# Products of ones through the first search of a transnormer-attention and balanced-MoE kernel

## The chip, the cores and the metric

The kernel runs on one core of one Trainium2 chip. The metric is the device time of one execution in microseconds (us). TensorE (PE in the profile) multiplies, VectorE (DVE) and ScalarE (ACT) work elementwise, GpSimd (POOL) also issues the indirect DMAs, SyncE (SP) issues the other DMAs. "Granted clock" is the share of TensorE's full clock that the profile records as granted.

## The reference

Two blocks follow one another. The first is a linear attention with normalised rows:

```python
kv = np.einsum('bhsd,bhse->bhde', k, v)            # batch 8, heads 8, seq 576, head_dim 64
out = np.einsum('bhsd,bhde->bhse', q, kv)
rms = np.sqrt(np.mean(out * out, axis=-1, keepdims=True) + 1e-06)
x = (out / rms * g_norm)                           # -> 4608 tokens of 512
```

The second gives every token to exactly one of 8 experts, greedily by the largest logit, with room for 576 tokens each:

```python
logits = x @ w_gate                                # [4608, 8]
for idx in np.argsort(-logits.flatten()):
    tok, e = idx // E, idx % E
    if assigned[tok] >= 0 or counts[e] >= cap: continue
    assigned[tok] = e; counts[e] += 1
for e in range(E):
    mask = assigned == e
    out[mask] = np.maximum(x[mask] @ w1[e], 0.0) @ w2[e]
```

## The kernel before, in words

**Attention.** For each of 8 batches `prepare` forms the key-value products (L397) and transposes the queries (L382), and `tiles` makes 4 or 5 tiles of 128 tokens (L481), squares them on ScalarE (L487), copies them out (L488), sums the squares on VectorE (L492), scales (L496 to L500) and reduces the logits (L505, L508). The last tile of the last batch is the end of TensorE's part in this phase. `choice` and `compare_thirds` (L295 to L305, L337) then bring the last quarter of the logits into the form that the search reads.

**PSUM.** The attention's PSUM pool is closed behind this, and a new one is opened for the experts. Its first two tiles are `given_ps` (one bank for all numbers that TensorE gives the search) and `held_ps` (one bank with small tables that VectorE reads). `held_ps` is filled at L598 to L604, which stand outside the hand-written order; VectorE's first instruction there is the copy at L598.

**The first search.** The greedy assignment is done one expert at a time: the largest logit value at which some expert is full is searched, that expert takes its tokens, and so on. The first search cannot lie beside any expert's products, because no expert has tokens yet. `threshold(0, ...)` runs six rounds (`s` from 0 to 5). In a round, TensorE counts for 32 candidate values how many tokens of each expert lie above them: 36 products at L653, one for each block of 128 tokens, with a weight tile of 128 x 32 and a moving tile of 128 x 8. VectorE turns the counts into one number for each candidate (L667, L669), TensorE sums that over the candidates with a matrix of ones and so hands it to all partitions (`kk`, L674), and VectorE works out the next candidates and compares all tokens with them, in three thirds of 12 blocks (L679, L317, L323 in rounds 1 to 3; L696, L337 in rounds 4 and 5), on which the next round's products wait third by third. Beside this, `lowest` has two small pairs of products (L618 behind the number of round 1, L621 behind that of round 2) whose results are needed later. `assign_first` then has two products (L736, L751), and `fetch(0)` makes the list of the first expert's tokens with three products (L919 to L921) and five (L938), from which the indices of the gather come (L950). GpSimd issues the gathers (L959).

**Products of ones.** `ones` (attention) and `warm` (experts) multiply a 128 x 128 tile of ones with a 128 x 512 tile of ones, in bfloat16, into a PSUM bank that nothing reads. Before the change `ones` stands ahead of and within the attention, and `warm(20)` stands behind the five products at L938, `warm(2)` twice behind the first two transposed blocks of tokens.

**Order.** In both blocks `tc.manual_schedule` keeps TensorE, VectorE and ScalarE (in the attention SyncE too) in the order of the program text. All waits between engines are put in by the framework. Each engine works through its own queue in order.

**Behind the search.** The first expert's products (L1149) begin when three gathered blocks of tokens are transposed (L1051) and copied (L1056). From there to the end TensorE works with few gaps, and the later searches lie beside the experts' products.

Of the kernel before, what the change touches and what calls it, by code (L numbers as in the profile page):

```python
# [7 lines left out]
FT = mybir.dt.float32  # L8
# [7 lines left out]
P = 128  # L16
# [10 lines left out]
def kernel(  # L27
# [11 lines left out]
    nc = tc.nc  # L39
# [4 lines left out]
    E, _, F = moe_w1.shape  # L44
# [105 lines left out]
    def small(nm, w=1, dt=FT):  # L150
        return asg.tile([P, w], dt, name=nm, tag="s_" + nm, bufs=2)
# [206 lines left out]
    def ones(times, to=None):  # L358

        if to is None:  # L360
            to = psa.tile([P, 512], FT, name="ones_ps", tag="tr", bufs=2)
        for _ in range(times):
            nc.tensor.matmul(to, lhsT=ones_b, rhs=wide, start=True, stop=True)
# [167 lines left out]
    with tc.manual_schedule(engines={PE, DVE, ACTE, SPE}):  # L531
        ones(18)
        for _ in prepare(0):
            pass
        for b in range(B):
            parts = prepare(b + 1) if b + 1 < B else iter(())
            rows = [((b, j), (b, j + 2)) for j in (0, 1, 4, 5)]
            if b % 2:
                rows.append(((b - 1, R - 1), (b, R - 1)))
            one, scale, logits = tiles(b // 2 * R + b % 2 * (R // 2), rows)  # L540
            copies = []
            if b in choose_at:
                early(*choose_at[b])
            for t in range(len(rows)):
                one(t, copies, {0: 1, 3: 2}.get(t, 0))
                next(parts, None)
                if b < 2 or t == 3 or b == 6 and t == 2:
                    chore()
            for _ in parts:
                pass  # L550
            if b + 1 == B:
                while chores:
                    chore()
            scale()
            logits()
            if b < B - 1:
                chore(2 if b == 6 else 1)

            while len(writes) >= 2 * LAG:
                writes.pop(0)()  # L560
        early(27, GC)
        while chores:
            chore()
        for do in late:
            do()
        while writes:
            writes.pop(0)()
# [35 lines left out]
    for n, x in enumerate((-0.5, 1.0 / QP, 0.0)):  # L603
        nc.vector.memset(one_more[:, n:n + 1], x)  # L604

    deferred = []

    floor = asg.tile([P, 1], FT, name="floor")
# [32 lines left out]
    def threshold(t, over, width, inv, mid):  # L641

        first = t == 0
        exact, ends, cand = first, None, None
        for s in range(NSTEP):
            last = s + 1 == NSTEP
            yield (4.6 if first else 2.8) if s > 0 else 0.4 if first else 2.4

            n_ps = small_ps["n"]
            if first:  # L650

                for c in range(GC):
                    nc.tensor.matmul(n_ps[0:QP, :, 0],  # L653
                                     lhsT=over[c // THIRD][:, c % THIRD],
                                     rhs=best[:, :, c], start=(c == 0), stop=(c == GC - 1))
            else:
                for c in range(0, GC, G):
                    nc.tensor.matmul(n_ps, lhsT=over[:, c:c + G].rearrange("p c n -> p (c n)"), rhs=best[:, :, c:c + G],  # L658
                                     start=(c == 0), stop=(c == GC - G))
            need = goal[0:QP]  # L660
            for g in range(1, 1 if first else G):
                less = small("need", E)[0:QP]
                nc.vector.tensor_tensor(less, need, n_ps[g * QP:(g + 1) * QP, :, g], op=AL.subtract)
                need = less
            full = small("full", E)[0:QP]
            n_full = small("n_full")[0:QP]
            nc.vector.scalar_tensor_tensor(full, in0=n_ps[0:QP, :, 0], scalar=0.0, in1=need, op0=AL.add,  # L667
                                           op1=AL.is_ge, accum_out=n_full)
            nc.vector.scalar_tensor_tensor(some[0:QP], in0=n_full.to_broadcast([QP, 3]), scalar=0.5, in1=one_more,  # L669
                                           op0=AL.is_gt, op1=AL.add)  # L670
            if not first:
                yield 4.0 if t == 1 and s == 0 else 1.7
            kk = small_ps["kk"]
            nc.tensor.matmul(kk, lhsT=ones_b, rhs=some, start=True, stop=True)  # L674
            exact = s + 1 >= DIGITS
            over = None if last else new_over(first)
            if s < DIGITS:
                mid_was, mid = mid, small("mid")
                nc.vector.tensor_scalar(mid, in0=kk[:, 0:1], scalar1=width[:, s:s + 1], scalar2=mid_was, op0=AL.mult, op1=AL.add)  # L679
                if not exact:  # L680
                    d = digits(mid, inv[:, s + 1:s + 2], None if first else small_ps["mx"])
                    if first:
                        for n in range(3):
                            compare_digits(over[n], d, marks, n * THIRD, (n + 1) * THIRD)
                    else:
                        compare_digits(over, d, small_ps["marks"])
                else:
                    lo = small("lo_at")
                    nc.vector.tensor_scalar(lo, in0=mid, scalar1=width[:, NSTEP:NSTEP + 1], scalar2=None, op0=AL.subtract)
            elif not last:  # L690
                ends = small("ends", 2)
                nc.vector.tensor_scalar(ends, in0=kk[:, 1:3], scalar1=width[:, s:s + 1], scalar2=lo, op0=AL.mult, op1=AL.add)
                lo = ends[:, 1:2]
            if exact and not last:
                cand = small("cand", NCAND + 2)
                nc.vector.tensor_scalar(cand[:, 0:NCAND + 1], in0=small_ps["row"], scalar1=width[:, s + 1:s + 2],  # L696
                                        scalar2=lo, op0=AL.mult, op1=AL.add)
                if first:
                    compare_thirds(over, cand)
                else:  # L700
                    compare(over, cand, 0, GC // 2)
                    yield 0.6
                    compare(over, cand, GC // 2, GC)
            if exact and s + 2 == NSTEP:
                nc.vector.tensor_copy(cand[:, NCAND + 1:NCAND + 2], ends[:, 0:1])
            if last:
                got = small("got_ends", 2)
                for n in range(2):
                    at = small("at", NCAND + 1)
                    nc.vector.scalar_tensor_tensor(at, in0=small_ps["row"], scalar=kk[:, 2:3], in1=cand[:, n:NCAND + 1 + n],  # L710
                                                   op0=AL.is_equal, op1=AL.mult, accum_out=got[:, 1 - n:2 - n])
                hi = small("hi")
                nc.vector.tensor_scalar(hi, in0=got[:, 0:1], scalar1=ends[:, 0:1], scalar2=None, op0=AL.min)
            if first:
                next(of_floor, None)
            if deferred:
                deferred.pop(0)()
        tops[t] = hi
        return hi, got[:, 1:2]

    def assign_first(ends):
# [12 lines left out]

        all_ps = small_ps["all"]
        nc.tensor.matmul(all_ps[:, 0:2].rearrange("p t e -> p (t e)"), lhsT=ones_b, rhs=sums, start=True, stop=True)  # L736
        edge = small("edge", GC)
        nc.vector.tensor_tensor(edge, cut[:, 1], cut[:, 0], op=AL.subtract)
        over_room = small_ps["over_room"]
# [9 lines left out]
        index = small("index", dt=I32)  # L749
        nc.vector.tensor_scalar(index, in0=which, scalar1=-1.0, scalar2=float(E), op0=AL.mult, op1=AL.add)  # L750
        nc.tensor.matmul(all_ps[:, 2, 0:1], lhsT=before, rhs=turn_of[:, GC - 1:GC], start=True, stop=True)  # L751
        nc.vector.tensor_tensor(room, room, all_ps[:, 0], op=AL.subtract)
        theirs, left = small("theirs", E), small("left_one")
        nc.vector.scalar_tensor_tensor(theirs, in0=code, scalar=which, in1=room,
# [132 lines left out]
                          mybir.DependencyInfo(mybir.DependencyClass.Sync, mybir.DependencyReason.DATA),  # L887
                          reason="TensorE waits for the tokens")

    def warm(times):  # L890
        w_ps = psm.tile([P, 512], FT, name="warm_ps", tag="y", bufs=2)
        for _ in range(times):
            nc.tensor.matmul(w_ps, lhsT=ones_b, rhs=wide, start=True, stop=True)

    def fetch(t, which, index, later):

        ch = choice() if 0 < t < E - 1 else iter(())
# [21 lines left out]
        nc.tensor.matmul(begin, lhsT=before, rhs=along[:, GC - 1:GC], start=True, stop=True)  # L919
        nc.tensor.matmul(a_ps[:, 1:GC + 1], lhsT=fall, rhs=along, start=True, stop=True)  # L920
        nc.tensor.matmul(a_ps[:, GC + 1:GC + 2], lhsT=prior, rhs=along[:, GC - 1:GC], start=True, stop=True)  # L921
        kn = know[:, t % 2]
        if t == 0:
            nc.scalar.copy(kn[:, 0:GC + 1], a_ps[:, 1:GC + 2])
# [13 lines left out]
            nc.tensor.matmul(s_ps[:, n], lhsT=since[:, n * P:(n + 1) * P], rhs=kn, start=True, stop=True)  # L938
        if t == 0:

            warm(20)
        rel_s = small("rel_s", NB)
        nc.vector.tensor_tensor(rel_s, place_f, s_ps[:, :, GC], op=AL.subtract)
        less = asg.tile([P, NB, GC], FT, name="less", tag="less")
# [388 lines left out]
```

## Time and profile before

| | |
|---|---|
| time, median of 3 runs (lowest, highest) | 655.35 us (655.14, 655.75) |
| the profiled execution: time, span of its instructions | 656.87 us, 655.1 us |
| mean granted clock | 0.964 |
| TensorE busy | 607.8 us (93%) |
| VectorE busy | 385.8 us (59%) |
| ScalarE, GpSimd busy | 195.0 us (30%), 391.1 us (60%) |
| the last products of the attention (L481) | start at 122.51 us |
| the first search, from the first counts to the indices | 125.0 to 154.5 us |
| granted clock 0.50 instead of 1.00 | 37.97 to 44.79 us and 123.30 to 157.43 us |

All times within the profile are counted from the start of the span. A row of the timeline has its start, the length, the engine, the line, the operation, output and inputs, the shapes and the number of instructions that were merged, and in brackets the idle time before it with what ended that. A row of the table of stretches has the stretch, its length, TensorE's busy time (instructions), the granted clock and the DMA engines' load.

### The profile page before, as it was taken

What the parts mean: (1) busy time and instruction counts of PE and PEld (TensorE: products, weight loads), DVE (VectorE), ACT (ScalarE), POOL (GpSimd) and SP (SyncE); (2) the same over time, 40 slices, a digit from 0 to 9 for tenths busy, and PEclk for the clock granted to TensorE, in tenths of its full rate; (3) what the DMA queues carried; (4) which work ended last, traced back from release to release, by engine and by line L of the source; (5) the groups of instructions that cost most, each with busy time, mean ns of one, the idle gap of its engine ahead of it and who ended that gap; (6) DMA issues with size and microseconds to landing.
All of it is one profiled execution on the core that took longest, in us unless ns stands there. A gap on an engine that the chain in (4) does not pass through costs nothing.

```text
span 655.1 us, 12759 instructions
## 1 busy us (share of the span) xinstructions
PE 607.8 (93%) x4922; PEld 467.4 (71%) x4939; DVE 385.8 (59%) x1242; ACT 195.0 (30%) x397; POOL 391.1 (60%) x407
## 2 busy tenths in 40 slices
PE   7889999346999999999999999999999999999994
PEld 4767777343778678867877786778678867877873
DVE  4456767877788678578747955975771153123101
ACT  1545556631331223123212322221223123222310
POOL 1134544204586488659747973887388579848822
PEclk9979999756999999999999999999999999999998
DMA  8998988324506403620631082109104520820001
GB/s 271 315 313 293 309 300 320 126 83 144 185 2 232 137 34 109 220 74 1 213 125 66 2 291 70 42 5 325 41 33 128 203 72 1 292 77 34 0 10 64
DMA packets 49884, 91.02 MB, mean 139 GB/s; under 512 B 3744, under 2 KB 20128, under 8 KB 49824
## 3 DMA queue, kind: packets, MB, share of 16 engines
q1 hardware_dynamic: 43200, 71.31, 31.8%
q0 software_dynamic: 5920, 18.88, 8.4%
q8 instruction: 39, 0.64, 0.4%
q14 instruction: 21, 0.17, 0.1%
q10 hardware_dynamic: 704, 0.02, 0.1%
HBM read 71.32 MB, written 18.87 MB: 138 GB/s over the span
## 4 chain that ended last, share of the span: by engine, by line
PE 77%; DVE 8%; DMA 6%; issue 4%; ACT 2%; POOL 1%; POOLq 0%; SPq 0%; DVEq 0%; ACTq 0%
PE x_ps L1149 13%; PE x_ps L1109 12%; PE z_ps L1149 9%; PE y_ps L1149 9%; PE y_ps L1109 8%; PE z_ps L1109 7%; DMA v_sb<-in_v_dram 4%; PE o_ps L481 4%; PE y_ps L1211 4%; PE t_ps L1051 3%; PE kv_ps L397 3%; PE qt_ps L382 2%; PE given_ps L658 1%; PE given_ps L653 1%; DMA q_sb<-in_q_dram 1%
## 5 line engine op out<-in xcount | busy, mean ns | idle before, releaser
L1154 ACT COPY h<-x_ps 128x288 f32<-128x288 f32 x93 | 37.2, 400 | 166.1 <-PE x_ps L1149 159.7
L1149 PE MATMUL x_ps<-xs,sw 128*128 128x288 f32 x248 | 71.4, 409 | 0.4 <-DVE xs L1064 0.4
L1076 POOL DMA_INDIRECT out_dram<-y_sb,outs x32 | 31.5, 983 | 56.6 <-DVE y_sb L1247 41.1
L1109 PE MATMUL x_ps<-tw,sh 128*128 128x256 f32 x256 | 61.5, 384 | 0.0
L1149 PEld LDWEIGHTS x_ps<-xs,sw 128*128 128x128 f32 x248 | 46.1, 190 | 13.4 <-issue 1.0
L1056 ACT ACTIVATE xt<-t_ps,g_col 128x512 f32<-128x512 f32 (+3 forms) x41 | 25.8, 635 | 91.1 <-PE t_ps L1051 90.9
L1101 POOL TENSOR_TENSOR sh<-hid 128x512 f32<-128x512 f32 x32 | 40.7, 1273 | 19.9 <-ACT hid L1124 19.9
L1109 PEld LDWEIGHTS x_ps<-tw,sh 128*128 128x128 f32 x256 | 47.0, 190 | 7.0 <-issue 0.8
L1037 POOL TENSOR_TENSOR sw<-w_sb 128x256 f32<-128x256 f32 x64 | 46.8, 731 | 7.9 <-PE z_ps L1149 7.5
L513 POOL TENSOR_TENSOR xo<-o_sb,inv 128x512 f32<-128x512 f32 x31 | 32.9, 1091 | 30.7 <-DVE inv L500 17.5
L1124 ACT ACTIVATE hid<-hid 128x576 f32<-128x576 f32 x64 | 43.8, 686 | 22.6 <-DVE hid L1163 12.6
L959 POOL DMA_INDIRECT xg<-x_dram,ids x40 | 37.9, 947 | 15.5 <-issue 9.8
L481 PE MATMUL o_ps<-kvx,qt 64*128 64x72 f32 (+1 forms) x640 | 39.7, 273 | 5.3 <-ACT o_sb L488 3.4
L1187 POOL TENSOR_TENSOR tw<-w_sb 128x512 f32<-128x512 f32 x32 | 40.1, 1277 | 6.5 <-DMA w_sb<-in_moe_w_dram 6.5
L481 PEld LDWEIGHTS o_ps<-kvx,qt 64*128 64x128 f32 (+1 forms) x640 | 34.4, 180 | 12.9 <-issue 8.1
L1149 PE MATMUL z_ps<-xt,sw 128*128 128x288 f32 x128 | 38.0, 414 | 0.0
L1149 PE MATMUL x_ps<-xt,w_sb 128*128 128x288 f32 x124 | 37.3, 415 | 0.5 <-ACT xt L1056 0.5
L1149 PE MATMUL y_ps<-xt,w_sb 128*128 128x288 f32 x128 | 36.8, 408 | 0.0
L1149 PE MATMUL z_ps<-xs,sw 128*128 128x288 f32 x128 | 36.8, 409 | 0.0
L1149 PE MATMUL y_ps<-xs,w_sb 128*128 128x288 f32 x128 | 36.5, 407 | 0.0
L492 DVE TENSOR_REDUCE ms<-sq 128x8 f32<-128x512 f32 x36 | 24.3, 682 | 20.4 <-ACT sq L487 20.1
L425 POOL COPY kvx<-kv 64x512 f32<-64x512 f32 x16 | 9.7, 608 | 44.2 <-DVE kv L419 24.7
(307 smaller groups left out, 1336.1 us busy)
## 6 DMA issues: line engine op xcount, KB each, us to landing
w_sb<-in_moe_w_dram SPq DMA_DIRECT2D x32, 512.0 KB, 5.5
w_sb<-in_moe_w_dram SPq DMA_DIRECT2D x8, 2048.0 KB, 12.6
k_sb<-in_k_dram SPq DMA_DIRECT2D x16, 576.0 KB, 5.5
v_sb<-in_v_dram SPq DMA_DIRECT2D x16, 576.0 KB, 5.9
q_sb<-in_q_dram SPq DMA_DIRECT2D x16, 576.0 KB, 5.6
x_dram<-xo SPq DMA_DIRECT2D x16, 512.0 KB, 4.3
x_dram<-xo SPq DMA_DIRECT2D x4, 256.0 KB, 3.7
xg<-x_dram,ids POOLq DMA_INDIRECT x40, 5.0
```

The lines of the kernel that those rows point to most:

```text
L481: nc.tensor.matmul(o_ps[rows_at, rp, (2 * r2 + l) * W:(2 * r2 + l + 1) * W], lhsT=turned_q[bn][ks, l, block // 2:block // 2 + m].rearrange ...
L513: nc.gpsimd.tensor_tensor(xo[:, t], o_sb[:, t, :, 0:D], inv[:, t * H:(t + 1) * H].rearrange("p (h o) -> p h o", o=1).to_broadcast([P, H, D ...
L959: tokens = nc.gpsimd.indirect_dma_start(out=xg[0:nr], out_offset=None, in_=x_dram, in_offset=bass.IndirectOffsetOnAxis(ap=ids[0:nr, n:n + ...
L1037: in_order(nc.gpsimd.tensor_tensor(o, x, y, op=op))
L1076: put = nc.gpsimd.indirect_dma_start(out=out, out_offset=bass.IndirectOffsetOnAxis(ap=ids_of[t][0:nr, n:n + 1], axis=0), in_=y_sb[0:nr, :] ...
L1101: in_order(nc.gpsimd.tensor_tensor(o[:, ms], x[:, ms], y[:, ms], op=op))
L1109: nc.tensor.matmul(p_ps[:, n], lhsT=left[:, f, n * P:(n + 1) * P], rhs=right[:, f], start=first, stop=(f == FH - 1), skip_group_check=True)
L1124: nc.scalar.activation(both, both, ACT.Relu)
L1149: nc.tensor.matmul(p_ps, lhsT=lhs[:, r], rhs=rhs[:, r], start=(m in (1, 2, 4, 5) and r == 0), stop=(r == 1), skip_group_check=(m in (6, 7, ...
L1154: nc.scalar.copy(u, p_ps)
L1187: in_order(nc.gpsimd.tensor_tensor(o, x, y, op=AL.subtract))
L1211: nc.tensor.matmul(y_ps[l * nr:(l + 1) * nr], lhsT=hid[:, l * FH + f, a:a + nr], rhs=w2[:, l * FH + f, :], start=(f == 0), stop=(f == FH - 1))
```

## The change

`warm` is defined earlier, and both helpers are called at eight places along the first search and its neighbours: seven products behind the last tile of the attention, ten ahead of the last nine counts of round 0, four behind each round's number (nine behind the last), three and five behind the two products of `assign_first`, two behind the three products at L919 to L921, and 24 instead of 20 behind those at L938. Nothing is taken away, and no value that is used changes.

```diff
             if b + 1 == B:
+                ones(7)
                 while chores:
                     chore()
...
+    def warm(times):
+        w_ps = psm.tile([P, 512], FT, name="warm_ps", tag="y", bufs=2)
+        for _ in range(times):
+            nc.tensor.matmul(w_ps, lhsT=ones_b, rhs=wide, start=True, stop=True)
...
                 for c in range(GC):
+                    if s == 0 and c == 27:
+                        warm(10)
                     nc.tensor.matmul(n_ps[0:QP, :, 0],
...
             nc.tensor.matmul(kk, lhsT=ones_b, rhs=some, start=True, stop=True)
+            if first:
+                warm(9 if last else 4)
...
         nc.tensor.matmul(all_ps[:, 0:2].rearrange("p t e -> p (t e)"), lhsT=ones_b, rhs=sums, start=True, stop=True)
+        warm(3)
...
         nc.tensor.matmul(all_ps[:, 2, 0:1], lhsT=before, rhs=turn_of[:, GC - 1:GC], start=True, stop=True)
+        warm(5)
...
         nc.tensor.matmul(a_ps[:, GC + 1:GC + 2], lhsT=prior, rhs=along[:, GC - 1:GC], start=True, stop=True)
+        if t == 0:
+            warm(2)
...
         if t == 0:
-            warm(20)
+            warm(24)
```

More of the change, by code (lines that the diff above doesn't have):

```diff
@@ L888, in behind @@
                           reason="TensorE waits for the tokens")
[L890 to L893, printed above, removed]
     def fetch(t, which, index, later):
```

## The prediction

> **What bounds the kernel now.** I read the page first (slices of the granted clock), then the chain of waits, then the timeline of the search, then a table of stretches. The clock drops only around the first search, and there the chain alternates between engines:
>
> ```profile
> PEclk9979999756999999999999999999999999999998
> ```
>
> ```profile
> 132.03 1.15 PE given_ps L653 x36
> 133.17 0.02 issue
> 133.20 0.17 DVE full L667 x2
> 133.37 0.02 issue
> 133.39 0.16 DVE some L669
> 133.55 0.04 issue
> 133.59 0.18 PE given_ps L674
> ```
>
> Each round is one loop without slack: candidates (L679, L317), first third of comparisons (L323), 36 counts (L653), their sums (L667, L669), the number (L674), candidates again. TensorE's part is 1.15 + 0.18 us of 2.85, all at half clock. What a full clock is worth there is read from the distance between counts, and from the one row of small products that runs at full clock (columns: start, length, engine, line):
>
> ```profile
> 132.03 1.13 PE L653 MATMUL given_ps<-best,over_c 128*32 128x8 bf16 x36 [1.12 <-DVE over_c L323]
> ...
> 164.81 0.38 PE L658 MATMUL given_ps<-best,over 128*128 128x32 bf16 x9
> ```
>
> The flight of one product is 0.175 us in both (175 and 176 ns). So 36 counts at half clock start (1.13 - 0.175) / 35 = 27 ns apart, and nine at full clock (0.38 - 0.176) / 8 = 25 ns apart: almost the same. The number's way is no shorter either: L674 to L679 takes 0.20 us at half clock (130.75 to 130.95) and 0.21 at full (170.11 to 170.32).
>
> When the clock falls and returns is in the table of stretches (start:end, length, TensorE busy, granted clock, DMA share, GB/s). The changes lie on a grid of 3.41 us: 37.97 to 44.79 is two of these, 123.30 to 157.43 ten.
>
> ```profile
> 34.55:37.97 3.42, 2.01 (x46) 1.00 0.92 300
> 37.97:41.38 3.41, 3.41 (x44) 0.50 0.99 324
> 41.38:44.79 3.41, 3.05 (x77) 0.50 1.00 356
> ...
> 116.47:119.89 3.42, 2.55 (x33) 1.00 0.38 145
> 119.89:123.30 3.41, 0.73 (x32) 1.00 0.65 246
> 123.30:126.71 3.41, 0.87 (x27) 0.50 0.02 6
> ...
> 154.02:157.43 3.41, 3.41 (x10) 0.50 0.72 226
> 157.43:160.85 3.42, 3.42 (x21) 1.00 0.64 200
> ```
>
> A stretch busy for 2.01 us lost the clock, one busy for 2.55 us kept it. Busy time counts an eight-column product's whole flight, so I also estimate the time in which columns stream (0.42 ns a bfloat16 column at full clock, twice that in float32, from the 288 columns of L1149 that start 242 ns apart): 0.39 of the stretch that lost it, 0.38 of the one that kept it. Upwards, 1.00 of products of ones brought it back at 157.43, and 0.65 in the first stretch of the kernel (0.42 to 3.83, 2.23 us busy with ones) did not: the ones behind it still start 0.427 apart. A 512-column product of ones takes 0.427 us at half clock (153.509 to 153.936) and 0.216 at full (157.826 to 158.042).
>
> **The change, part by part.** All sums are shifts of the gather's start (155.30). Behind it the chain is a DMA and then TensorE's products, so each us carries to the end.
>
> *Gain of a full clock.* Three rounds of 36 counts fed by L323: 35 x 1.7 ns and 0.02 for the first, 0.08 each. Two rounds fed by L337, whose last third comes late: 0.035 each. The nine counts 0.03, the five at L938 0.04. Sum 0.38 us. Lower bound 0. Upper bound, if 32-column weights went at half of 27 ns: the last third of comparisons then ends last, 0.26 x 3 + 0.16 x 2 + 0.12 + 0.07 = 1.3 us. I take the 25 ns of L658, the only full-clock row of such products.
>
> The Trainium skill, "TensorE: Matmul & The Clock Gate", section "LDWEIGHTS (loading the stationary operand)", estimates a load at its columns / 1.2 ns, with no clock in the formula, so 27 ns for 32 columns; by it this gain is nil.
>
> *Seven behind the last tile.* They start at about 123.1. The stretch that ends at 123.30 is not altered (0.73 us busy), so the clock still falls there: one at 0.216, six at 0.427, the last starts at 125.43 and lands 0.634 later, at 126.07. Who waits for that:
>
> ```profile
> 123.93 0.69 DVE L492 TENSOR_REDUCE ms<-sq 128x8 f32<-128x512 f32 x1 [0.26 <-ACT sq L487]
> 125.01 0.23 DVE L598 COPY held_ps<-rise 128x72 f32<-128x72 f32 x1 [0.39 <-ACT o_sb L488]
> 125.30 0.40 DVE L497 RECIPROCAL inv<-rt 128x40 f32<-128x40 f32 x1
> ```
>
> L598 writes the new pool's second bank, which L488 does not read, yet it waits for the last L488: the whole old pool must be free. The seven use the old pool, so L598 waits for them too, and behind it on VectorE stand L497 to L508, L295 to L305 and L337, the chain up to the nine counts at 129.90. L598 goes at about 126.11 instead of 125.01: 1.10 us. Bounds: 0, if the clock were full (seven end at 124.8, before L488's 124.98) or if the framework puts L598 to L604, which stand outside the manual order, behind L500; 1.10 as the order stands. I take 1.10. The 27 early counts wait as well, 125.03 to 126.2, and have cover.
>
> *Ten ahead of the nine counts.* Ones fill 2.7 us of 123.30 to 126.71, 0.79, between the 0.65 that did not bring the clock back and the 1.00 that did; I take it as back at 126.71. Then the ten end at 129.1, and the nine counts are due at 131.0: nothing. At half clock they would end at 131.2: 0.2.
>
> *Four behind each number.* At full clock 0.86 us, where TensorE waits 1.28 (kk at 133.59 to counts at 134.88): hidden. But does the clock hold? In 130.13 to 133.54 there are four (0.86) and the columns of some 36 counts (0.12): 0.29 of the stretch, below the 0.38 that kept the clock. Busy time, 0.4 + 0.17 + 1.03 + 0.41 with the nine counts at 131.0, is 2.0 us, as much as where it fell. I take it to fall at 133.54, behind the second number.
>
> The Trainium skill, the same page, section "Why this matters for your kernels", says that the clock is lost by idle gaps of over about 3 us. The row differs: 37.97 came after a longest recorded gap of 1.48 us (34.48 to 35.96). By that rule the filled search would stay at full clock, and the sum would be 1.10 - 0.38 = +0.7.
>
> At half clock four take 1.71 us. Behind round 1's number, with L618's two products (2 x 0.22): 2.15 against 1.28, 0.87 late. Round 2, with L621 (0.4): 0.83. Round 3: 1.71 against 1.73, nothing. Round 4: 1.71 against 1.48, but the last third is compared 0.93 after the first, and TensorE catches up: nothing.
>
> *Nine behind the last number.* At full clock 1.94 us against a wait of 2.77 (146.21 to 148.99): hidden. At half 3.84: 1.07 late. The nine are longer than a stretch, so the clock should return within them; between 0 and 1.07 I take 0.70.
>
> *Three, five, two, 24.* L736 to L751 is 1.40 us, L751 to L919 1.74, L921 to L938 0.77. At full clock they take 0.65, 1.08, 0.43: hidden. At half, five cost 0.40 and two 0.1; I take 0. The 24 at full clock end 5.2 us behind L938, the third gathered block came 8.6 behind it (161.55): hidden. Without that cover (half clock) four more cost up to 0.6.
>
> *Sum.* 1.10 + 0.87 + 0.83 + 0.70 = 3.50, less 0.10 of the gain (only a quarter of the search at full clock): +3.4 us. The profiled execution (656.87 us, of which the span is 655.1) would become 660.3. It lies 1.5 us above the median of the runs, 655.35; on that median the sum gives 658.8. Own range of this case: +2.0 (L598 moved behind L500 and part of the nine hidden) to +4.4 (nine in full, five as well), 657.4 to 659.8.
>
> **The rivals.**
>
> *Fill hidden throughout, clock full* (chance 0.16): L598 is placed late or the seven run fast, and a 0.29 share holds the clock. Then -0.38, 655.0; down to 654.0 if counts go at half of 27 ns. This decides from the point at which 130.13 to 133.54 ends at 1.00. For it: at 0.216 each, every run of ones fits into the wait it stands in. Against it: 123.30 falls whatever follows.
>
> *The clock holds, but L598 is late* (0.18): 1.10 - 0.38 = +0.7, 656.1. For it: the flights of counts may count as activity. Against it: the 2.01 us row.
>
> *The clock hardly returns* (0.08): ten cost 0.2, round 0's four 0.43, rounds 1 and 2 as above, nine in full, five 0.40, 24 some 0.5: 1.10 + 0.2 + 0.43 + 0.87 + 0.83 + 1.07 + 0.40 + 0.5 = +5.4, 660.8.
>
> **How the numbers follow.** Likeliest case 0.58: 658.8. 0.2% is 1.3 us, about what a measurement of this kernel can tell from no change. Faster by more needs the first rival and counts at half of 27 ns: 0.07. Within it lie the rest of that rival and the second: 0.27. Slower: 0.58 + 0.08 = 0.66. The range goes from 655.0, the first rival's middle, to 660.0, above the likeliest case's end; outside lie half of the first rival and the third, 0.16.
>
> **What would show it.** Right: L598 starting near 126.1 with TensorE's ones as what ended its wait; a clock of 0.50 in a stretch between 133 and 150; counts of rounds 2 and 3 that start some 2.1 us behind their number, with no wait for VectorE; L736 released by TensorE's queue, not by VectorE. Wrong: L598 at 125.0 or behind L500; 1.00 from 127 on, with counts 13 ns apart; the gather starting before 155.3.

## The result, and the profile after

Over 22 runs of each, the kernel after takes 660.26 us (median; 657.33 to 669.57) and the kernel before 656.30 us (653.52 to 668.98). The ratio is 1.0059, 95% interval 1.0040 to 1.0077: slower by 0.6%, about 3.9 us. The profiled execution of after takes 663.41 us, with a span of 661.5 us.

All of it that belongs to the change lies between the last tile of the attention (L481) and the list's products (L938 before, L947 after; the lines behind L549 have moved): 30.44 us before, 34.56 us after, +4.12 us. From there to the first expert's products it is 9.83 and 9.92 us. From those to the end it is 492.3 us before and 494.7 in this execution of after, but 492.2 to 492.4 us in the profiles of the first five experiments, two of which have exactly after's products behind the list; the 2.4 us are this execution's own.

The page's 40 slices of the granted clock show the same three low slices around the search, with 8, 5 and 8 tenths instead of 7, 5 and 6:

```profile
PEclk9979999858999999999999999999999999999998
```

VectorE's timeline of after, at the point where the attention's PSUM pool is closed:

```profile
123.81 0.69 DVE L492 TENSOR_REDUCE ms<-sq 128x8 f32<-128x512 f32 x1 [0.26 <-ACT sq L487]
125.98 0.24 DVE L599 COPY held_ps<-rise 128x72 f32<-128x72 f32 x1 [1.49 <-PE ones_ps L363]
126.13 0.39 DVE L497 RECIPROCAL inv<-rt 128x40 f32<-128x40 f32 x1
```

The copy now waits for products of ones, and starts 3.60 us behind L481 instead of 2.50. Some 0.14 us of the 1.10 come back just behind it (L497 starts 0.15 us behind the copy, before the change 0.29), so the nine counts are 0.96 late.

TensorE's timeline of after, rounds 0 to 2 and the end of the search:

```profile
123.04 2.83 PE L363 MATMUL ones_ps<-wide,ones_b 128*128 128x512 bf16 x6
...
126.76 2.35 PE L610 MATMUL warm_ps<-wide,ones_b 128*128 128x512 bf16 x10
130.73 0.40 PE L661 MATMUL given_ps<-best,over_c 128*32 128x8 bf16 x9 [1.62 <-DVE over_c L337]
131.57 0.16 PE L682 MATMUL given_ps<-some,ones_b 128*128 128x3 bf16 x1 [0.44 <-DVE some L677]
131.81 0.81 PE L610 MATMUL warm_ps<-wide,ones_b 128*128 128x512 bf16 x3
132.85 1.12 PE L661 MATMUL given_ps<-best,over_c 128*32 128x8 bf16 x36 [0.23 <-DVE over_c L323]
134.41 0.16 PE L682 MATMUL given_ps<-some,ones_b 128*128 128x3 bf16 x1 [0.43 <-DVE some L677]
134.43 1.87 PE L610 MATMUL warm_ps<-wide,ones_b 128*128 128x512 bf16 x4
136.23 0.58 PE L624 MATMUL f_ps<-ident,low 128*1 128x128 f32 x2
136.61 1.15 PE L661 MATMUL given_ps<-best,over_c 128*32 128x8 bf16 x36
...
149.12 4.00 PE L610 MATMUL warm_ps<-wide,ones_b 128*128 128x512 bf16 x9
152.92 0.22 PE L746 MATMUL given_ps<-sums,ones_b 128*128 128x16 bf16 x1
```

A few records of ones are missing (x3 for four). Round 1 still waits for VectorE: the four behind number 0 are hidden. From number 1 on nothing in brackets stands before the counts: they start behind the ones and L624, 2.20 us after their number instead of 1.28. L746 starts 3.82 us behind the last number, where before it was 2.77. The chain of waits says the same, with TensorE's own queue in the place of the candidates and comparisons, and ahead of L746 it has the nine:

```profile
134.57 1.73 PE warm_ps L610 x4
136.30 0.51 PE f_ps L624 x2
136.82 0.96 PE given_ps L661 x36
```

The table of stretches of after (start:end, length, TensorE busy, granted clock, DMA share, GB/s) shows where the clock was:

```profile
120.01:123.43 3.42, 1.05 (x33) 1.00 0.58 220
123.43:126.84 3.41, 3.25 (x34) 0.50 0.00 1
126.84:130.25 3.41, 2.27 (x10) 1.00 0.01 2
130.25:133.67 3.42, 2.20 (x44) 1.00 0.39 153
133.67:137.08 3.41, 2.98 (x35) 0.50 0.36 136
...
147.32:150.73 3.41, 2.98 (x42) 0.50 0.01 2
150.73:154.15 3.42, 3.20 (x9) 0.50 0.00 0
154.15:157.56 3.41, 2.75 (x20) 1.00 0.22 50
```

It came back for 6.8 us only, 126.84 to 133.67, and then stayed at half until 154.15, behind L746.

Delays along the search, in us (start to start):

| step | before | after | late by | predicted |
|---|---|---|---|---|
| L481 to the nine counts | 7.39 | 8.35 | 0.96 | 1.10 |
| round 1 (number 0 to number 1) | 2.85 | 2.84 | 0 | 0 |
| round 2 | 2.85 | 3.80 | 0.95 | 0.87 |
| round 3 | 2.85 | 3.90 | 1.06 | 0.83 |
| rounds 4 and 5 | 6.93 | 6.99 | 0.06 | 0 |
| last number to L746 | 2.77 | 3.82 | 1.05 | 0.70 |
| L746 to L762 | 1.40 | 1.47 | 0.07 | 0 |
| gain of a full clock | | | none | -0.10 |

### The profile page after: what moved, and what is told of

It is laid out like the page before. It is cut to its first block, busy times and chain, and to the rows that moved or that the text cites. A ratio compares the mean times of both kernels' runs of the same rounds, so it can differ in the third digit from the quotient of the medians.

```text
span 661.5 us, 12874 instructions
## 1 busy us (share of the span) xinstructions
PE 625.2 (95%) x4977; PEld 472.6 (71%) x4999; DVE 385.8 (58%) x1242; ACT 194.8 (29%) x397; POOL 390.9 (59%) x407
## 4 chain that ended last, share of the span: by engine, by line
PE 81%; DVE 7%; issue 4%; DMA 2%; ACT 2%; POOL 1%; POOLq 0%; SPq 0%; DVEq 0%; ACTq 0%
PE x_ps L1158 13%; PE x_ps L1118 11%; PE z_ps L1158 9%; PE y_ps L1158 8%; PE y_ps L1118 7%; PE z_ps L1118 7%; PE o_ps L481 5%; PE y_ps L1220 4%; PE kv_ps L397 3%; PE t_ps L1060 3%; PE warm_ps L610 2%; PE qt_ps L382 2%; DMA v_sb<-in_v_dram 2%; PE given_ps L666 1%; PE given_ps L661 1%
## 5 line engine op out<-in xcount | busy, mean ns | idle before, releaser
L481 PE MATMUL o_ps<-kvx,qt 64*128 64x72 f32 (+1 forms) x640 | 39.5, 273 | 5.2 <-ACT o_sb L488 3.4
L481 PEld LDWEIGHTS o_ps<-kvx,qt 64*128 64x128 f32 (+1 forms) x640 | 34.2, 180 | 12.7 <-issue 7.8
```

Source lines behind the costliest of these rows:

```text
L481: nc.tensor.matmul(o_ps[rows_at, rp, (2 * r2 + l) * W:(2 * r2 + l + 1) * W], lhsT=turned_q[bn][ks, l, block // 2:block // 2 + m].rearrange ...
```

## The experiments

The theory is that of the prediction: ones that run at half clock are longer than the waits they stand in, the copy at L598 waits for the seven, and a full clock is worth little to the search. Rivals: the cost lies in the seven alone, or in the mere number of products, or a clock that was really held would shorten the search. Before's median stood between 654.2 and 654.7 us in the timed sessions of the experiments.

| kernel | ratio to before (95%) | L481 to list, against before's 30.44 us |
|---|---|---|
| seven alone | 1.0029 (0.9997 to 1.0062) | +1.14 |
| all but the seven | 1.0048 (1.0019 to 1.0078) | +3.48 |
| sized for half clock | 1.0011 (0.9978 to 1.0043) | +0.49 |
| clock held throughout | 1.0005 (0.9971 to 1.0038) | -0.05 |
| fours alone | 1.0060 (1.0029 to 1.0090) | +3.17 |

**The seven alone.** Before, with this one line:

```diff
             if b + 1 == B:
+                ones(7)
                 while chores:
```

> The kernel before with the seven products of ones behind the last tile alone. Theory (the seven hold back the first copy into the new PSUM pool, and fills that run at half clock do the rest): from the last tile's products to the nine counts of round 0 the way is 0.96 us longer, as in the changed kernel (8.35 against 7.39); the clock returns at the first grid point behind (some 126.8) and falls again at the next (130.2), as nothing follows the seven; the rest of the search takes as long as before, the whole +1.0 us. Rival (all of the cost comes from the fills between the numbers): 0 us, the copy starts 2.5 us behind the last tile's products.

VectorE's timeline of this kernel:

```profile
124.46 0.24 DVE L599 COPY held_ps<-rise 128x72 f32<-128x72 f32 x1 [1.70 <-PE ones_ps L363]
```

L481 starts at 120.65 here, so the copy is at +3.81 and the nine counts at +8.54; all later distances are before's. The cost is 1.14 us and not 0.96, since the clock fell earlier in the seven, at 121.48, 0.17 us behind their start (121.31) instead of 0.39. The time's interval reaches from nothing to 0.6%, so it is the trace and not the time that shows this term.

**All but the seven.** After, with `ones(7)` taken out.

> The changed kernel without the seven behind the last tile. Theory: the first copy into the new pool starts 2.5 us behind the last tile's products again; without the seven the clock is not back when the ten run, so that they end about 130.2 instead of 129.9 due (0.3 late); it is back for round 0's four, falls one stretch later, and rounds 1 and 2 and the last number are late by 0.9, 1.06 and 1.05 as in the changed kernel: +3.2 to +3.4 against before. Rival (the seven are the whole cost, all else is hidden): +0.3 or less.

VectorE's timeline, then TensorE's, of this kernel:

```profile
124.82 0.23 DVE L598 COPY held_ps<-rise 128x72 f32<-128x72 f32 x1 [0.39 <-ACT o_sb L488]
```

```profile
125.65 4.42 PE L609 MATMUL warm_ps<-wide,ones_b 128*128 128x512 bf16 x10
130.00 0.40 PE L660 MATMUL given_ps<-best,over_c 128*32 128x8 bf16 x9
```

The copy waits for ScalarE alone again, +2.50 as before. But the stretch from 123.09, where the clock fell, has ones only from 125.65 on and does not bring it back: the ten run at half clock until 129.91 and hold the nine counts up by 0.30 us. Behind that every delay is after's (number to counts 1.28, 2.21, 2.33, 1.82, 1.82; last number to L746 3.82), and the search is 3.48 us longer, just above the 3.2 to 3.4 expected. So the seven's own wait and the later delays are separate terms, but the two kernels' costs (1.14 and 3.48) don't add to 4.12 exactly: without the seven the ten pay instead, and the clock fell at another point of the program in each (0.77 to 1.05 us behind the start of L481).

**Sized for half clock.** After, with each run short enough for its wait at 0.427 us a product:

```diff
-                ones(7)
+                ones(3)
...
-                        warm(10)
+                        warm(8)
...
-                warm(9 if last else 4)
+                warm((2, 1, 1, 3, 2, 6)[s])
...
-        warm(5)
+        warm(3)
...
-            warm(2)
+            warm(1)
...
-            warm(24)
+            warm(20)
```

> The changed kernel with every run of ones cut so that it fits its wait even at half clock: 3 instead of 7, 8 instead of 10, behind the numbers 2, 1, 1, 3, 2 and 6 instead of 4, 4, 4, 4, 4 and 9, three instead of five, one instead of two, 20 instead of 24. Theory (the cost is nothing but ones that outlast their wait): the search from the last tile's products to the five at the list takes 30.4 us as before, within 0.2, and the time is that of before within noise. Rival (a fill costs also where it fits: weight loads, bank changes, the queue): each of ten places costs some 0.05 to 0.1, the search 31 us or more.

TensorE's timeline of this kernel at the last tile, then VectorE's at the copy:

```profile
124.31 1.24 PE L481 MATMUL o_ps<-kvx,qt 64*64 64x72 f32 x32 [2.98 <-ACT o_sb L488]
```

```profile
127.32 0.24 DVE L599 COPY held_ps<-rise 128x72 f32<-128x72 f32 x1 [0.39 <-ACT o_sb L488]
```

TensorE's timeline in round 2, with a single product of ones at half clock:

```profile
135.89 0.16 PE L682 MATMUL given_ps<-some,ones_b 128*128 128x3 bf16 x1 [0.44 <-DVE some L677]
135.91 0.59 PE L610 MATMUL warm_ps<-wide,ones_b 128*128 128x512 bf16 x1
136.43 0.59 PE L624 MATMUL f_ps<-ident,low 128*1 128x128 f32 x2
137.17 1.13 PE L661 MATMUL given_ps<-best,over_c 128*32 128x8 bf16 x36
```

Number to counts is 1.28 again, and all distances are before's except the first: +0.49 ahead of the nine counts, which is outside the 0.2 that was expected. That is no wait for the ones: here the clock had fallen at 123.92, before L481 began at 124.31, so the last attention products ran at half clock themselves (1.24 us instead of 0.73), and the copy waited for ScalarE, not for ones. The fours alone, which have no ones there, show the same +3.01 us from L481 to the copy. The extra products as such cost nothing where they fit.

**Clock held throughout.** After, with more ones at most places, so many that the clock does not fall in the search:

```diff
+                if b + 1 == B and t + 1 == len(rows):
+                    ones(9)
...
-                        warm(10)
+                        warm(15)
...
+            if first:
+                warm(2)
             kk = small_ps["kk"]
...
-                warm(9 if last else 4)
+                warm((5, 4, 4, 7, 6, 12)[s])
...
-        warm(3)
+        warm(5)
...
-        warm(5)
+        warm(7)
```

> The changed kernel with so many ones that the clock should never fall in the search: nine more ahead of the last tile's products, 15 instead of 10, two ahead of each number, behind the numbers 5, 4, 4, 7, 6 and 12, five and seven within the assignment. All are sized to fit at full clock. Theory A (a full clock gives these products nothing, because the counts start 26.5 ns apart at either clock in the changed kernel): clock 1.00 from 60 to 160 us, the search 30.3 to 30.5 us, the time of before within noise. Theory B (a held clock is worth the predicted 0.38 us): 30.0. Theory C (dense ones slow the search by themselves): over 30.8 with the clock at 1.00. If the clock falls all the same, over 34 us.

The table of stretches of this kernel, then TensorE's timeline in round 2:

```profile
120.00:140.00 20.00, 17.95 (x226) 1.00 0.28 108
140.00:160.00 20.00, 19.65 (x190) 1.00 0.20 68
```

```profile
137.04 1.02 PE L612 MATMUL warm_ps<-wide,ones_b 128*128 128x512 bf16 x4
138.00 0.38 PE L626 MATMUL f_ps<-ident,low 128*1 128x128 f32 x2
138.30 1.12 PE L663 MATMUL given_ps<-best,over_c 128*32 128x8 bf16 x36
```

At full clock four take 1.02 us and every delay is gone: the theory's first half. And the search takes 30.39 us, 0.05 less than at half clock: what the products of ones were to buy is worth almost nothing, because 36 counts take 1.12 us at full clock and 1.13 to 1.15 at half.

**Fours alone.** Before, with `warm(4)` behind the numbers of rounds 0 to 4:

```diff
             nc.tensor.matmul(kk, lhsT=ones_b, rhs=some, start=True, stop=True)
+            if first and not last:
+                warm(4)
```

> The kernel before with nothing but the four products of ones behind the numbers of rounds 0 to 4. Theory (the same four cost at half clock what outlasts the wait, and fours alone do not bring the clock back): clock 0.50 through the rounds; from a number to the next counts 1.8, 2.2, 2.3, 1.8, 1.8 us instead of 1.28, 1.28, 1.28, 1.73, 1.48; the last two give their late start back, as the third part of the comparisons is late itself; the search +2.5 us. So round 0's four, which cost nothing in the changed kernel at full clock, cost 0.5 here. Rival (the cost of a four does not hang on the clock): round 0 stays at 1.28 us, or all rounds are late by the same.

TensorE's timeline of this kernel, round 1:

```profile
127.92 0.16 PE L679 MATMUL given_ps<-some,ones_b 128*128 128x3 bf16 x1 [0.43 <-DVE some L674]
128.32 1.49 PE L609 MATMUL warm_ps<-wide,ones_b 128*128 128x512 bf16 x3 [0.24 <-issue]
129.74 1.15 PE L658 MATMUL given_ps<-best,over_c 128*32 128x8 bf16 x36
```

The clock was 0.50 from 118.74 to 156.29, all through the search. Rounds 1 to 3 are then late by 0.56, 0.96 and 1.07 us, the last two by 0.07. Of +3.17, 0.51 lies ahead of the copy (L481 at half clock) and the fours' own are 2.66, close to the 2.5 expected. So fours alone, on a fallen clock, cost more than the seven; and the one reason that round 1 is not late in after is that its four still ran at full clock.

**The pace of small products.** Before, with 48 products of ones of each of six shapes, in two passes ahead of the attention, ones between them:

```diff
+    def pace():
+        to = psa.tile([P, 512], FT, name="pace_ps", tag="tr", bufs=2)
+        for w, n in ((32, 8), (64, 8), (128, 8), (32, 32), (32, 64), (8, 8)):
+            for _ in range(48):
+                nc.tensor.matmul(to[0:w, 0:n], lhsT=ones_b[:, 0:w], rhs=wide[:, 0:n], start=True, stop=True)
+            ones(2, to)
```

> The kernel before with a measurement ahead of its first products and again behind the 18 products of ones there: 48 products each with weights of 32, 64, 128 columns and 8 moving ones, of 32 columns and 32 and 64 moving ones, and of 8 columns and 8 moving ones, all ones, into a bank that nothing reads, with two ones between. The start is some 15 us later; only the distances count. Theory A (the load of the weights sets the pace and runs at 1.2 columns a ns at either clock): 26.7 ns for 32 columns and 53 for 64 at half and at full clock alike, 64 moving columns 53 at half and 27 at full, and 8 weight columns below 26. Theory B (a floor of some 25 ns for one product at either clock, the load runs with the clock): 64 columns 53 at half and some 27 at full, 8 columns some 25.

TensorE's timeline of this kernel; the first two rows are at half clock, the last two at full (a product of ones between them lasts 0.61 us in the first pair, 0.38 in the second):

```profile
1.61 1.42 PE L372 MATMUL pace_ps<-wide,ones_b 128*32 128x8 bf16 x48 [1.61 <-DVE wide L99]
3.92 2.72 PE L372 MATMUL pace_ps<-wide,ones_b 128*64 128x8 bf16 x48 [0.36 <-issue]
...
19.81 1.35 PE L372 MATMUL pace_ps<-wide,ones_b 128*32 128x8 bf16 x48
21.64 1.68 PE L372 MATMUL pace_ps<-wide,ones_b 128*64 128x8 bf16 x48
```

By their recorded starts, without the first spacing of each row, products with weights of 32 columns go every 26.6 ns at half clock and every 25.0 at full; those with 64 columns every 53.3 and every 31.7. So the load of 64 columns follows the clock, while 32 columns gain only 1.6 ns; 8 columns at full clock go every 25.1, no faster, so 25 ns is a floor here. That is theory B of the text, except that it expected some 27 for 64 columns at full clock. Wider is not slower throughout: in the rows of 128 columns the products go every 26.7 and 25.1 ns, as with 32; no run here shows why.

**The operands of the counts.** Before, with five runs of 36 products at full clock: plain; with moving columns 36 elements apart, as `best[:, :, c]` has them; accumulating; with changing weights; all three.

```diff
+        for far, more, other in ((0, 0, 0), (1, 0, 0), (0, 1, 0), (0, 0, 1), (1, 1, 1)):
+            for n in range(36):
...
+                nc.tensor.matmul(to[0:32, 0:8], lhsT=wide[:, 32 * x:32 * x + 32], rhs=apart[:, :, n if far else 0] if far else wide[:, 0:8],
```

> The kernel before with a measurement behind the first 18 products of ones, at full clock: five times 36 products with weights of 32 columns and 8 moving columns, first as in the measurement before (25.1 ns apart at full clock), then with the moving columns 36 elements apart, then accumulating into one place, then with other weights from product to product, then all three as the search has them; six ones behind each. Only the distances count. The counts of the search start 26.65 ns apart at a clock that stayed full. Theory A (an operand of the search's form costs the 1.5 ns): one of the three variants, and the last, show 26.5 to 27. Theory B (it isn't the form): all show 25.1, and the reason stays open.

TensorE's timeline of this kernel, plain, columns apart, and all three:

```profile
7.19 1.05 PE L374 MATMUL pace_ps<-wide 128*32 128x8 bf16 x36
9.57 1.12 PE L374 MATMUL pace_ps<-wide 128*32 128x8 bf16 x36
...
16.80 1.12 PE L374 MATMUL pace_ps<-wide 128*32 128x8 bf16 x36
```

By the recorded starts, again without the first spacing, 25.0, 26.6 and 26.65 ns, as theory A of the text expected: the strided moving operand makes 1.6 ns, and accumulating or changing weights nothing (25.0 each). So the counts of the search, at 26.7 ns under either clock, lose at full clock through their operand what they would have gained from it.

## Why the prediction fell short

The direction, the place of every delay and the order of events were as predicted: the copy released by the ones, the clock back where the ten begin and lost again between the numbers of rounds 0 and 1, rounds 2 and 3 late with no wait for VectorE, L746 behind TensorE's queue, the ten and the three, five, two and 24 hidden but for 0.07. The sum was too small, 3.4 against 4.1, and it stood on a base that was too low; together they put 660.26 just above the range. That the sum laid on the profiled execution (656.87 us) gave 660.3 is luck: that base was 0.6 us above before's median of 22 runs, and the sum about as much too small.

- **"Nine behind the last number … I take 0.70" is the term most mis-sized: 1.05 us.** Its reason, "the nine are longer than a stretch, so the clock should return within them", failed. The nine take 3.84 us, but they began 1.8 us into a stretch of the grid (149.12 in 147.32 to 150.73) whose first part was a round of counts; its share of streaming columns, estimated as in the prediction, is 0.56, and it did not bring the clock back. The next stretch, which the nine and the three behind them filled, ended at 154.15, when the nine were over. So a run longer than a stretch need not bring the clock back while it lasts: these nine were split, 1.6 us into one stretch and 2.2 into the next.
- **Rounds 2 and 3** (0.87 and 0.83 predicted) came to 0.95 and 1.06. That the four run at half clock with a pair behind them was right; but the four hold the queue for 1.80 us (134.43 to 136.23), not 1.71, and the pair at L627 for 0.51, not 0.4.
- **The gain of 0.10** was nothing. It was built on the 25 ns of L658, whose moving operand comes in runs of four neighbouring elements (`best[:, :, c:c + G]`, G = 4), where the counts take single elements 36 apart; the counts themselves ran only at half clock before, so no row of before could show it. The runs give 26.67 ns before, 26.69 after and 26.65 with the clock held.
- **L598's 1.10** was 1.10 at the copy and 0.96 at the nine counts; the step left out that the distance from L598 to L497 shrinks from 0.29 to 0.15 us when the copy waits for the ones.
- **The clock's rows.** "The clock drops only around the first search" is too narrow: it was low from 37.97 to 44.79 as well, and from 648.95 on, where TensorE had nothing left to do. The fall that the text puts behind the second number lies ahead of it by its own times, as it did in the run. The sum does not rest on either.
- **The base.** The sum was laid on 655.35 us, a median of three runs that agreed within 0.6 us. Over 22 runs before has 656.30, from 653.5 up; this 0.95 us was not in the range. The shift itself, 3.9 us by the times and 4.1 by the trace, lies within the case's own +2.0 to +4.4.

Of the rivals, "clock full" needed a clock worth 0.38 us: with the clock held it was worth 0.05. "The clock holds" failed at 133.67. "The clock hardly returns" was wrong for the ten, the five and the 24, right for the nine.

The place where the prediction weighed the Trainium skill, "TensorE: Matmul & The Clock Gate", section "LDWEIGHTS (loading the stationary operand)", is worth a second look. Its load time without a clock gave a gain of nil, which is what was measured, but not for that reason: 64 columns went from 53.3 to 31.7 ns when the clock rose, so for 32 and 64 columns the formula describes the half clock; the pace kernel's 128 columns (26.7 ns at half clock, 25.1 at full) it fits at neither. And for its section "Why this matters for your kernels", idle gaps as what loses the clock, the pace kernel has a row that differs, in its table of stretches:

```profile
22.40:25.81 3.41, 3.18 (x90) 2.70 (x91) 0.00 (x0) 0.00 (x0) 0.00 (x0) 1.00 0.60 215
25.81:29.22 3.41, 2.97 (x63) 2.38 (x62) 0.00 (x0) 0.00 (x0) 0.00 (x0) 0.50 0.03 10
```

TensorE was busy for 3.18 of 3.41 us, by eight-column products mostly, and lost the clock behind it.

## What to carry to other kernels

Before products are added to keep a clock, measure the spacing of the products that should gain from it at both clocks: here it was 26.7 ns under either, and a clock held from end to end saved 0.05 us of a search of 30. Filling must be sized by what it takes when the clock has already fallen, because a run that just fits its wait at full clock takes twice as long just then (0.427 us a product against 0.216); sized so, it cost nothing that the runs here can tell. Filling that writes to a PSUM pool about to be closed delays the first use of the next pool: 1.10 us for seven products.

## What the runs showed of the hardware

- **The clock fits the columns streamed better than busy time.** This is an estimate, with 0.42 ns a bfloat16 column at full clock, 0.83 at half and twice that in float32. In after, stretches with a share of 0.61 kept the clock and one with 0.23 lost it (2.20 us busy); the pace kernel lost it at some 0.24 (3.18 us busy). At half clock, shares of 0.53 to 0.64 in after did not bring it back, 0.7 (123.43 to 126.84) and nearly 1.0 (150.73 to 154.15) did. In before, 37.97 to 41.38 was busy throughout, at some 0.67, and did not. The bounds are blurred: the prediction's rows have 0.39 that lost the clock and 0.38 that kept it, and no run was made to find them more closely.
- **The grid of 3.41 us is not tied to the program.** The clock fell 0.79 us behind the start of L481 in before, 1.05 in after, 0.83 and 0.77 in the first two experiments, but 0.39 and 0.43 ahead of it in the third and the fifth, whose programs are alike up to the last tile. So the cost of the same line differs between executions by tenths of a us (seven: 0.96 and 1.14), and one profile of a kernel shows one such position.
- **A strided moving operand costs 1.6 ns a product** at eight columns 36 elements apart, measured only at full clock, against the 25.0 ns of the same products without the stride.
